# Attention and two expert layers on one core: one transposition for both heads' odd 64 keys, first keys by head, a planner that counts tiling changes and shared access, new ranks

## The chip, the cores and the metric

One core of a Trainium2 chip runs the whole program. The metric is the device time of one execution in microseconds (us). PE is the matrix engine, with PEld its weight loads; DVE, ACT and POOL are the vector, scalar and general engines, and SP issues most of the transfers. All engines work through their own instruction lists in order and wait for each other by semaphores.

## The reference

Attention over 2 batches of 8 heads, 576 positions, head size 64, in float32; its output goes through two expert layers.

```python
def _attn_ref(q, k, v):            # q, k, v: 2, 8, 576, 64
    ...
    q_rot, k_rot = (rotate(q), rotate(k))
    scores = (1.0 / np.sqrt(D)) * np.matmul(q_rot, k_rot.transpose(0, 1, 3, 2))
    attn = np.exp(scores - np.max(scores, axis=-1, keepdims=True))
    attn = attn / (np.sum(attn, axis=-1, keepdims=True) + 1e-09)
    return np.matmul(attn, v).astype(np.float32)

x = attn_out.transpose(0, 2, 1, 3).reshape(1152, 512)
h = x @ w_in;  x = (h * np.tanh(softplus(h))) @ w_out              # 512 -> 2048 -> 512
h = x @ w2_in; x = (P(h) / Q(h)) @ w2_out                          # the same sizes
```

## The kernel before

Attention goes pair by pair: eight pairs, each the two heads `2j` and `2j+1` of one batch. For a pair, `load` brings q, k and v, `turned` rotates q and k (`rope.1` to `rope.4`, on POOL for all pairs but the first, whose work is shared between DVE and POOL), and `columns` transposes them on PE and lets ACT and DVE split them into a high and a low part (`turn`, `turn.hi`, `turn.lo`). `score` multiplies queries by keys for a tile `t` of 128 query rows. For `t` 0 to 3 the two heads stand in the upper and lower 64 rows of PE and run side by side (12 matmuls of 288 columns); `t` = 4 holds the last 64 rows of both heads (6 matmuls over all 128 rows). DVE takes the row maxima (`score.max`), ACT the exponentials (`score.exp`). `turn_p` transposes the exponentials (`p.turn`), ACT and DVE take turns in copying the result out (`p.move`, `p.move2`), `weigh` multiplies it by the values, two heads in the two column halves of PE, and `shares` divides by the sums (`sum.turn`, `sum.spread`, `x.scale`, and `x.hi`, `x.lo` on POOL).

576 keys are four blocks of 128 and 64 odd ones. The four blocks of each head are transposed one by one; the odd 64 of the first head go to rows 0 to 63 of the transposed block `PTr`, those of the second head to rows 64 to 127, by two transpositions and two copies for each tile (L611, L612).

The expert layers follow (`up`, L807, and `down`, L891). Their weights come as 64-bit words, and `prepare` takes each half of a block apart: `w.size` (ACT), `w.bound`, `w.shift`, `w.low` (DVE), `w.hi` (ACT), `w.lo` (DVE). The first halves are prepared while attention still runs.

What sets the order is a planner, `Plan.emit`. Every operation has a cost in a table of formulas, and the planner plays the program through: of all operations that are ready it issues the one that can start first, after adding the operation's number in `YIELD`, and breaks ties by its place in the program plus its number in `EARLY_LATE`. It also hands out the eight PSUM banks (`Banks(1)`, `Banks(2)`). The order that comes out is fixed in the program.

Of the kernel before, what the change touches and what calls it, by code (L numbers as in the profile page):

```python
# [42 lines left out]
def pool(n, wide=False):  # L43
# [3 lines left out]

EARLY_LATE = {
    "down.add": 1136, "g.hi": -2317, "g.lo": 6461, "g.low": -15, "load": 762, "mish": 8083, "p.move": 2011,
    "p.turn": 31, "ratio.10": -108, "ratio.11": -2315, "ratio.2": -4968, "ratio.3": -593, "ratio.4": 423,  # L50
    "ratio.5": -1752, "ratio.6": 4202, "ratio.7": -3763, "ratio.8": 10584, "rope.1": -2749, "rope.2": 22,
    "rope.4": -2386, "score": -3812, "score.max": 3118, "start": -1592, "store": 1136, "sum.inv": 7595, "sum.lo":
    4253, "sum.row": 510, "sum.spread": -2329, "sum.turn": -7911, "turn": -370, "turn.lo": -3170, "up": -2124,
    "w.bound": -442, "w.hi": -117, "w.keep": -380, "w.lo": 426, "w.load": -689, "w.low": -124, "w.shift": -4497,
    "w.size": -2423, "weigh": 378, "x.hi": 924, "x.lo": 3178, "x.scale": 1155, "y.hi": 91, "y.lo": -3805}
# [4 lines left out]
    "down": 2368, "down.add": 703, "g.hi": 1295, "g.lo": 447, "g.low": 585, "mish": 850, "p.move": 218, "p.turn":  # L60
    481, "ratio.1": 120, "ratio.10": 228, "ratio.2": 48, "ratio.4": 2226, "ratio.5": 196, "ratio.6": 442,
    "ratio.7": 3284, "ratio.8": 485, "ratio.9": 549, "rope.1": 601, "rope.2": 1192, "rope.3": 501, "rope.4": 146,
    "score": 49, "score.max": 252, "sum.inv": 985, "sum.lo": 49, "sum.row": 196, "sum.spread": 430, "sum.turn":
    453, "turn.lo": 409, "up": 2286, "w.bound": 219, "w.hi": 859, "w.keep": 237, "w.lo": 1062, "w.load": 718,
    "w.low": 1007, "w.shift": 411, "w.size": 1921, "weigh": 1097, "x.scale": 105, "y.hi": 1745, "y.lo": 446}
# [16 lines left out]
class Plan:  # L82
# [3 lines left out]
    def __init__(self):  # L86
        self.ops = []
        self.write = {}
        self.reads = {}
        self.live = []  # L90
        self.turns = {}
        self.rank = []
        self.names = []

# [7 lines left out]
    def op(self, name, engine, cost, fn, r=(), w=(), late=0.0, after=()):  # L102
# [28 lines left out]
        self.names.append(name)  # L131
        self.ops.append((engine, cost, fn, deps, order - deps - {i}, late, banks))
        return i

    def emit(self, banks=8):
# [36 lines left out]
        users = {}  # L172

# [18 lines left out]
        while len(issued) < n:  # L192
            rooms = {}
            best = None
            for engine, group in ready.items():
                for i in group:
                    t = max(free[engine], at[i])
# [16 lines left out]
            issued.append(i)  # L214
            places = list(rooms[takes[i]][1]) if takes[i] else []
# [18 lines left out]
def block_kernel(ctx: ExitStack, tc: tile.TileContext, q, k, v, w1_in, w1_out, w2_in, w2_out,  # L234
# [211 lines left out]

    def load(p, n, queue=None):
# [6 lines left out]
        def main(h, e):  # L454
            i = src[b, 2 * j + h, 0:512, :]
            if n == "v":
                e.dma_start(out=vm[:, h].rearrange("p t d -> p (t d)"), in_=i.rearrange("(p t) d -> p (t d)", t=4))
            else:
                e.dma_start(out=t[:, 0:4, h, :], in_=i.rearrange("(p t) d -> p t d", t=4))  # L459

        def end(a, e):

            if n == "k":
                e.dma_start(out=last[0:64], in_=src[b, 2 * j:2 * j + 2, 512:S, :].rearrange("h p d -> p h d"))
            else:
# [9 lines left out]
        if p < 2:  # L475
            plan.op("start", "POOL", 300 if n == "k" else 600, zero, w=[(x, "z")])
        for h in range(2):
            dma([(x, h)], lambda e, h=h: main(h, e), 131e3, queue)
        for a in range(1 if n == "k" else 2):
            dma([(x, "e", a)], lambda e, a=a: end(a, e), 32e3 if n != "k" else 64e3, queue)  # L480
# [511 lines left out]
```

## Time and profile before

| | |
|---|---|
| time of three runs | median 576.4 us (576.3 to 576.94) |
| the profiled execution | 574.76 us, of which the span of the profile is 573.0 us |
| busy in the span | PE 547.1, PEld 495.2, DVE 459.1, ACT 373.4, POOL 102.5 us |
| busy in the chain that ended last | PE 89%, POOL 2%, DVE 2%, ACT 2% of the span |
| the expert layers' matmuls alone | L807 204.0 us and L891 201.9 us of PE |

The profiled execution is 1.76 us longer than its span, and 1.64 us shorter than the median of the runs. Until about 13 us the first keys and queries are loaded and turned, until about 175 us the eight pairs go through, and from there on the expert layers run.

### The profile page before, as it was taken

Reading aid. Unit: us, or ns where it says so; the run is one execution under the profiler, and the core shown is the slowest. Engines: PE = TensorE matmul, PEld = TensorE weight load, DVE = VectorE, ACT = ScalarE, POOL = GpSimd, SP = SyncE. Lnnn points to the kernel's source line nnn. Section 1 sums busy time; section 2 is a strip of 40 time slices with the busy share of each in tenths; the row PEclk is TensorE's granted clock in tenths of the full one; section 3 lists DMA queues with packets and bytes.
Section 4 is the critical chain, followed back from the end, with each engine's and each line's share of the span. In section 5 each row is a group of like instructions: output and inputs, shape, how many; then the busy total and the mean of one; then the engine's idle time right before and its main releaser. Section 6 shows DMA issues by size and latency. Waiting matters only on the chain.

```text
span 573.0 us, 8774 instructions
## 1 busy us (share of the span) xinstructions
PE 547.1 (95%) x3416; PEld 495.2 (86%) x3416; DVE 459.1 (80%) x629; ACT 373.4 (65%) x555; POOL 102.5 (18%) x100
## 2 busy tenths in 40 slices
PE   3998899799999999999999999999999999999997
PEld 2776676677689999999999999999998988999985
DVE  4778787877766866987876869789889989998993
ACT  2867584776766856686754788666765767655560
POOL 7979897302112000000000000000000000000000
PEclk9999899999999999999999999999999999999999
DMA  5434402201226192769292961503404300300004
GB/s 146 92 77 115 124 22 74 76 12 31 74 74 222 40 399 81 283 225 369 76 360 79 350 237 78 216 1 146 148 0 145 150 0 5 142 2 0 1 18 148
DMA packets 38681, 69.35 MB, mean 121 GB/s; under 512 B 22256, under 2 KB 24560, under 8 KB 37104
## 3 DMA queue, kind: packets, MB, share of 16 engines
q1 hardware_dynamic: 37296, 68.43, 34.2%
q8 instruction: 27, 0.44, 0.3%
q10 hardware_dynamic: 1344, 0.36, 0.3%
q14 instruction: 14, 0.11, 0.1%
HBM read 53.84 MB, written 14.94 MB: 120 GB/s over the span
## 4 chain that ended last, share of the span: by engine, by line
PE 89%; POOL 2%; DVE 2%; SPq 2%; ACT 2%; DMA 1%; issue 1%; POOLq 0%; DVEq 0%; ACTq 0%
PE banks L807 35%; PE banks L891 35%; PE banks L657 6%; PE banks L608 5%; PE banks L564 4%; ACT f L580 1%; DVE f L577 1%; PE banks L521 1%; PE banks L683 1%; POOL f L499 1%; SPq L466 1%; POOL f L500 1%; SPq L459 1%; PE banks L611 1%; PE banks L612 1%
## 5 line engine op out<-in xcount | busy, mean ns | idle before, releaser
L807 PE MATMUL banks<-r 128*128 128x384 f32 x1152 | 204.0, 334 | 0.0
L891 PE MATMUL banks<-r 128*128 128x384 f32 (+1 forms) x1008 | 201.9, 358 | 0.0
L807 PEld LDWEIGHTS banks<-r 128*128 128x128 f32 x1152 | 200.3, 188 | 0.8
L891 PEld LDWEIGHTS banks<-r 128*128 128x128 f32 x1008 | 181.0, 188 | 16.4
L580 ACT ACTIVATE f<-banks,f 128x576 f32<-128x576 f32 x72 | 52.9, 741 | 26.3 <-DVE f L577 25.6
L577 DVE TENSOR_REDUCE f<-banks 128x1 f32<-128x576 f32 x72 | 52.0, 751 | 17.7 <-PE banks L564 17.4
L564 PE MATMUL banks<-r 64*128 64x288 f32 (+1 forms) x432 | 45.8, 323 | 4.6 <-ACT f L580 3.7
L564 PEld LDWEIGHTS banks<-r 64*128 64x128 f32 (+1 forms) x432 | 36.9, 198 | 13.5 <-ACT f L580 6.0
L849 ACT ACTIVATE f<-banks 128x768 f32<-128x768 f32 x24 | 19.6, 815 | 44.1 <-PE banks L807 44.1
L897 DVE TENSOR_TENSOR x<-banks,x 128x384 f32<-128x384 f32 (+1 forms) x63 | 37.3, 610 | 10.3 <-PE banks L891 10.1
L657 PE MATMUL banks<-x,f 128*64 128x256 f32 (+1 forms) x320 | 42.4, 411 | 0.0
L833 DVE TENSOR_TENSOR r<-f,r 128x768 fp32r<-128x768 f32 x24 | 22.8, 957 | 22.1 <-ACT r L829 22.0
L630 DVE COPY x<-banks 128x512 f32<-128x512 f32 (+2 forms) x64 | 31.9, 504 | 10.6 <-PE banks L608 7.4
L608 PE MATMUL banks<-f 128*128 128x128 f32 x288 | 38.7, 277 | 1.5 <-ACT f L580 1.5
L854 DVE TENSOR_TENSOR f<-f 128x768 f32<-128x768 f32 x24 | 23.0, 959 | 17.5 <-ACT f L852 17.4
L332 ACT ACT_TABLE_LOAD x28 | 35.9, 1283 | 0.5
L608 PEld LDWEIGHTS banks<-f 128*128 128x128 f32 x288 | 31.6, 141 | 4.8 <-ACT f L580 2.0
L657 PEld LDWEIGHTS banks<-x,f 128*64 128x64 f32 x320 | 22.6, 136 | 14.2 <-issue 2.3
L626 ACT COPY x<-banks 128x512 f32<-128x512 f32 (+1 forms) x56 | 28.4, 525 | 9.3 <-PE banks L608 8.6
L829 ACT ACTIVATE f<-banks 128x768 f32<-128x768 f32 x24 | 19.4, 813 | 19.9 <-PE banks L807 19.8
L817 ACT CAST r<-f 128x768 fp32r<-128x768 f32 x24 | 19.5, 824 | 14.7 <-DVE f L865 14.7
L852 ACT ACTIVATE f<-f 128x768 f32<-128x768 f32 x24 | 24.7, 1030 | 2.3 <-DVE f L865 1.6
(78 smaller groups left out, 694.1 us busy)
## 6 DMA issues: line engine op xcount, KB each, us to landing
f<-in_moe_w_in SPq DMA_DIRECT2D x16, 1024.0 KB, 5.1
f<-in_moe_w_out SPq DMA_DIRECT2D x16, 1024.0 KB, 5.9
outside<-f SPq DMA_DIRECT2D x12, 1024.0 KB, 4.7
r<-outside SPq DMA_DIRECT2D x12, 1024.0 KB, 6.6
f<-in_v SPq DMA_DIRECT2D x16, 128.0 KB, 2.1
out<-x SPq DMA_DIRECT2D x8, 256.0 KB, 2.5
x<-in_k SPq DMA_DIRECT2D x14, 128.0 KB, 3.0
x<-in_q SPq DMA_DIRECT2D x8, 128.0 KB, 3.0
```

Source lines behind the costliest of these rows:

```text
L332: nc.scalar.preload_act_table_set(name)
L564: nc.tensor.matmul(bank(Ps[h])[:, hf, 0:HW], qT[r, x, t * 128:(t + 1) * 128], kT[r, y, hf * HW:(hf + 1) * HW], start=(n == 0), stop=(n == 2))
L577: nc.vector.tensor_reduce(nm, bank(P)[:, :, 0:HW], axis=AX.XY, op=ALU.max, negate=True)
L580: nc.scalar.activation(view(e.off, 2, HW), bank(P)[:, :, 0:HW], AF.Exp, bias=nm, accum_out=sm)
L608: nc.tensor.transpose(bank(P)[:, kb * 128:(kb + 1) * 128], x[:, kb * 128:(kb + 1) * 128], idf)
L626: nc.scalar.copy(o, i)
L630: nc.vector.tensor_copy(o, i)
L657: nc.tensor.matmul(bank(P)[64 * a:64 * a + 64, 0:n], l, r, start=(kb == 0), stop=(kb == 4), skip_group_check=True)
L807: nc.tensor.matmul(bank(P)[:, i, 0:BW], y[:, cb, f], x[:, cb, tok], start=(cb == 0 and n == 0), stop=(cb == CB - 1 and n == 2))
L852: plan.op("ratio.2", "ACT", act(N, False, 2), lambda: nc.scalar.activation(q_, a, AF.Identity, bias=prm[:, 4:5], scale=prm[:, 5:6]), r=[(b ...
L891: nc.tensor.matmul(bank(P)[:, 0:n], x, y, start=(f == 0 and j == 0), stop=(f == FT - 1 and j == 2))
L897: nc.vector.tensor_tensor(total(), bank(P)[:, 0:n], total(), ALU.add)
```

## The change

1. The exponentials of the two heads now lie side by side in one buffer of 1152 columns, so that the first head's last 64 keys and the second head's first 64 keys are neighbours. One transposition of these 128 columns and one copy fill `PTr` for both heads. The second head's blocks begin 64 keys later, and its values are loaded in the matching order, in four transfers where there was one and an end (`load`, `ENDS`).
2. The tile `t` = 4 is transposed in one group: ten transpositions of 64 rows, the two heads in the upper and lower rows of PE, into two banks (L664, L666, L667), where there were four of 128 and two odd ones.
3. The last 64 keys of a pair are transposed with all 128 rows instead of 64.
4. The first pair's keys are loaded head by head in one piece of 1 KB for each partition, one head by ACT's queue and one by SP's, and rotated head by head (`turned_first`); the first pair's other loads change queues, and the keys' end is transposed alone (`"f"`).
5. The planner adds 95 ns to an operation of PE whose tiling differs from the one before (`DIVIDE`, `form`), and lets no two operations of the list `SHARED` overlap. Some costs of PE's operations change with it.
6. `EARLY_LATE` and `YIELD` have other numbers throughout.

```diff
+DIVIDE = 95.0
+
+SHARED = {"rope.1", "rope.2", "rope.3", "rope.4", "x.hi", "x.lo", "w.bound", "w.shift", "w.low", "w.lo", "g.low", "g.lo", "ratio.3",
+          "ratio.9", "ratio.10", "ratio.11", "y.lo"}
...
-    "down.add": 1136, "g.hi": -2317, "g.lo": 6461, "g.low": -15, "load": 762, "mish": 8083, "p.move": 2011,
+    "down": 1720, "down.add": 895, "g.hi": -113, "g.lo": -913, "g.low": 4029, "load": 1697, "mish": 300, "p.move":
...
-                    t = max(free[engine], at[i])
+                    t = max(free[engine] + DIVIDE * (engine == "PE" and self.form[i] != divided), at[i])
+                    if names[i] in SHARED:
+                        t = max(t, shared)
...
-                e.dma_start(out=t[:, 0:4, h, :], in_=i.rearrange("(p t) d -> p t d", t=4))
+                e.dma_start(out=vm[:, h] if (n, p) == ("k", 0) else t[:, 0:4, h, :], in_=i.rearrange("(p t) d -> p t d", t=4))
...
+    def turned_first(x, b1, b2, engine):
...
+        for h in (1, 0):
+            for name, b, f in (("rope.1", b1, c), ("rope.2", b2, s)):
+                plan.op(name, engine, dve(256), lambda h=h, b=b, f=f: eng.tensor_tensor(
+                    view(b.off, 4, 4, 32)[:, :, 2 * h:2 * h + 2], view(x.off, 2, 4, 2, 32)[:, h], f, ALU.mult),
+                    r=[(x, h), ROPE_T], w=[(b, h)])
...
-        e = T["P", p, i] = plan.ring("P", PR, S, 6)
+        e = T["P", p, t] = plan.ring("P", PR, 2 * S, 3)
...
-            if a is not None:
-                x = view(es[a][0].off, S)
+            if t == 4:
+                x = view(es[0].off, 64 + S)
+                rs = slice(0, 64), slice(64, 128)
                 for kb in range(4):
-                    nc.tensor.transpose(bank(P)[:, kb * 128:(kb + 1) * 128], x[:, kb * 128:(kb + 1) * 128], idf)
+                    for h, r in enumerate(rs):
+                        nc.tensor.transpose(bank(P)[:, h, kb * 64:kb * 64 + 64],
+                                            x[r, 64 + 64 * h + kb * 128:64 + 64 * h + (kb + 1) * 128], idf[r, r])
+                nc.tensor.transpose(bank(P)[0:64, 0, 256:320], x[rs[0], S:S + 64], idf[rs[0], rs[0]])
+                nc.tensor.transpose(bank(P)[:, 1, 256:320], x[rs[1], 0:128], idf[rs[1], rs[1]])
                 return
-            for i in range(m):
-                nc.tensor.transpose(bank(P)[0:64, i * 128:(i + 1) * 128], view(es[0][i].off, S)[:, 512:S], idf)
-                nc.tensor.transpose(bank(P)[:, (m + i) * 128:(m + i + 1) * 128], view(es[1][i].off, S)[:, 448:S], idf)
+            for i, e in enumerate(es):
+                x = view(e.off, 2 * S)
+                k = [512] if a is None else [(S + 64) * a + kb * 128 for kb in range(4)]
+                for n, f in enumerate(k):
+                    nc.tensor.transpose(bank(P)[:, (i + n) * 128:(i + n + 1) * 128], x[:, f:f + 128], idf)
...
+        keys, last_keys = load(0, "k", nc.scalar)
+        queries, last_queries = load(0, "q", nc.scalar)
         dma([ROPE_T], lambda e: e.dma_start(out=tab, in_=rope), 164e3)
-        load(0, "k", nc.scalar)
-        load(0, "q")
-        dma([("idf",)], lambda e: e.dma_start(out=idf, in_=ident), 64e3, nc.scalar)
+        last_keys(0, nc.scalar)
+        keys(1, None)
+        keys(0, nc.scalar)
+        dma([("idf",)], lambda e: e.dma_start(out=idf, in_=ident), 64e3)
+        queries(0, nc.scalar)
+        queries(1, None)
```

How the rows move is read from the two programs' instruction lists. On PE, in the middle of attention of the program before: a run of 24 score matmuls, the spreading of the sums (L683, L685), transpositions of exponentials (L608, with L611 and L612 for the odd keys), and the next pair's keys and queries (L521).

```order
L564 MATMUL banks<-r 128x288 x24
L683 MATMUL banks<-r 128x128 x4
L685 MATMUL banks<-r 128x64 x2
L608 MATMUL banks<-f 128x128 x12
L611 MATMUL banks<-f 64x128
L612 MATMUL banks<-f 128x128
L611 MATMUL banks<-f 64x128
L612 MATMUL banks<-f 128x128
L564 MATMUL banks<-r 128x288 x12
L521 MATMUL banks<-f,x 128x128 x9
L521 MATMUL banks<-f,x 128x64
```

A pair's round in the changed program, a little earlier in attention (L618 are the score matmuls, L673 all transpositions of whole tiles, L664 to L667 those of `t` = 4, L571 those of keys and queries, L719 the product with the values):

```order
L618 MATMUL banks<-r 128x288 x24
L673 MATMUL banks<-f 128x128 x14
L618 MATMUL banks<-r 128x288 x18
L673 MATMUL banks<-f 128x128 x8
L664 MATMUL banks<-f 128x64 x8
L666 MATMUL banks<-f 64x64
L667 MATMUL banks<-f 128x64
L673 MATMUL banks<-f 128x128 x4
L571 MATMUL banks<-f,x 128x128 x10
L719 MATMUL banks<-x,f 64x256 x10
```

The pairs of L611 and L612 are gone, the group of ten for `t` = 4 stands behind a run of 18, and all ten transpositions of the next pair's keys and queries have 128 rows.

On ACT, at the start of the program before (loads of the first keys, of the identity, the table of functions, and the first split):

```order
L459 DMA x<-in_k 128x4x64 x2
L464 DMA x<-in_k 64x2x64
L712 DMA f<-c_ident 128x128
L713 ACT_TABLE_LOAD
L530 ACTIVATE r<-banks 128x512
```

In the changed program:

```order
L782 ACT_TABLE_LOAD
L481 DMA x<-in_k 128x256
L481 DMA x<-in_q 128x4x64
L486 DMA x<-in_k 64x2x64
L583 ACTIVATE r<-banks 128x64
```

The table of functions is now loaded ahead of the three transfers, the keys' end is third, and the first split is that of the keys' end; the second head of the keys stands second in SP's list.

On DVE, where the second half of the first expert weights is taken apart during attention (L394 `w.bound`, L397 `w.shift`, L400 `w.low`), the program before has:

```order
L630 COPY x<-banks 64x64 x2
L394 TENSOR_SCALAR f<-f 128x1024
L577 TENSOR_REDUCE f<-banks 128x1
L397 TENSOR_SCALAR f<-f 128x1024
L400 SCALAR_TENSOR_TENSOR f<-f 128x1024
L577 TENSOR_REDUCE f<-banks 128x1 x4
```

The same three steps in the changed program (L410, L413, L416; L632 are the maxima, L752 is `x.scale`, L759 `sum.lo`):

```order
L632 TENSOR_REDUCE f<-banks 128x1 x2
L759 TENSOR_TENSOR r<-banks,r 9x128
L410 TENSOR_SCALAR f<-f 128x1024
L413 TENSOR_SCALAR f<-f 128x1024
L416 SCALAR_TENSOR_TENSOR f<-f 128x1024
L632 TENSOR_REDUCE f<-banks 128x1
L752 TENSOR_TENSOR f<-f,banks 128x576
```

They have moved from the fifth pair's maxima to those of the seventh pair, and stand in one piece.

## Rows read from the trace of the kernel before

**Rows 1.** Busy time by stretch: each engine's busy us and instructions, PE's granted clock, DMA.

```profile
12.98:171.00 158.02, 146.09 (x1242) 114.35 (x1242) 121.68 (x210) 107.75 (x261) 89.94 (x71) 0.99 0.25 68
50.00:64.00 14.00, 9.71 (x75) 7.80 (x75) 12.11 (x18) 8.02 (x19) 13.61 (x11) 0.88 0.34 100
175.00:390.00 215.00, 215.00 (x1238) 214.45 (x1238) 169.26 (x215) 150.82 (x161) 3.48 (x2) 1.00 0.55 204
```

**Rows 2.** Timeline of PE, 33.5 to 39 us: start us, duration us, instruction, idle before.

```profile
34.08 1.85 PE L564 MATMUL banks<-r 64*128 64x288 f32 x24
36.95 0.94 PE L521 MATMUL banks<-f,x 128*128 128x128 f32 x6 [1.02 <-POOL f L503]
```

**Rows 3.** Costliest groups: count, busy us, mean ns of one, idle before them.

```profile
L580 ACT ACTIVATE f<-banks,f 128x576 f32<-128x576 f32 x72 | 52.9, 741 | 26.3 <-DVE f L577 25.6
```

**Rows 4.** Timeline of DVE and PE around 100 us, then DVE at 137 us.

```profile
97.81 1.25 DVE L397 TENSOR_SCALAR f<-f 128x1024 int32<-128x1024 int32 x1
...
99.09 2.46 DVE L400 SCALAR_TENSOR_TENSOR f<-f 128x1024 int32<-128x1024 int32 x1
...
103.14 0.66 PE L683 MATMUL banks<-r 128*128 128x128 f32 x4 [2.96 <-ACT f L580]
...
137.37 0.68 DVE L397 TENSOR_SCALAR f<-f 128x1024 int32<-128x1024 int32 x1
```

**Rows 5.** Timeline of PE at 60 us.

```profile
60.46 3.40 PE L564 MATMUL banks<-r 128*128 128x288 f32 x18 [2.17 <-ACT f L580]
```

**Rows 6.** Timeline of PE, 25 to 30 us.

```profile
25.08 0.27 PE L521 MATMUL banks<-f 128*128 128x128 f32 x1
25.29 0.27 PE L521 MATMUL banks<-f,x 64*128 64x64 f32 x1
...
28.25 1.04 PE L608 MATMUL banks<-f 128*128 128x128 f32 x8
29.12 0.27 PE L611 MATMUL banks<-f 128*64 128x128 f32 x1
...
29.65 1.07 PE L564 MATMUL banks<-r 64*128 64x288 f32 x12
```

**Rows 7.** Timeline of the first 13 us, all engines and queues.

```profile
0.75 1.32 ACTq L459 DMA_DIRECT2D x<-in_k  x2
...
2.10 0.65 ACTq L464 DMA_DIRECT2D x<-in_k  x1
...
3.44 1.28 ACT L713 ACT_TABLE_LOAD   x1 [3.44 <-issue]
...
5.29 0.69 DVE L499 TENSOR_TENSOR f<-x,f 128x512 f32<-128x512 f32 x1 [4.32 <-DMA x<-in_k]
...
7.57 0.50 POOL L501 TENSOR_TENSOR x<-f 128x64 f32<-128x64 f32 x1
...
7.92 0.43 DVE L499 TENSOR_TENSOR f<-x,f 128x256 f32<-128x256 f32 x1
...
7.95 1.12 PE L521 MATMUL banks<-f,x 128*128 128x128 f32 x4 [7.95 <-DMA f<-in_q]
...
10.06 0.68 DVE L536 TENSOR_TENSOR r<-banks,r 128x512 fp32r<-128x512 f32 x1
...
12.98 3.25 PE L564 MATMUL banks<-r 64*128 64x288 f32 x24
```

**Rows 8.** Issues of transfers: count, size of each, median us from issue to landing.

```profile
f<-in_moe_w_out SPq DMA_DIRECT2D x16, 1024.0 KB, 5.9
...
f<-in_v SPq DMA_DIRECT2D x16, 128.0 KB, 2.1
...
x<-in_k ACTq DMA_DIRECT2D x2, 128.0 KB, 3.2
```

**Rows 9.** Timeline of PE at the end of attention.

```profile
167.38 4.44 PE L807 MATMUL banks<-r 128*128 128x384 f32 x24
171.75 2.38 PE L657 MATMUL banks<-x,f 128*64 128x256 f32 x20
```

More of the change, by code (lines that the diff above doesn't have):

```diff
@@ L52 @@
[L52 to L55, printed above, removed]
-YIELD = {
[L60 to L65, printed above, removed]
+    "down": 1720, "down.add": 895, "g.hi": -113, "g.lo": -913, "g.low": 4029, "load": 1697, "mish": 300, "p.move":
@@ new lines @@
+    458, "p.turn": 3152, "ratio.1": -256, "ratio.10": 1560, "ratio.11": 519, "ratio.2": -70, "ratio.3": 3622,
+    "ratio.4": -1438, "ratio.5": 1161, "ratio.6": -1346, "ratio.7": 5516, "ratio.8": -122, "ratio.9": -499,
+    "rope.1": 622, "rope.2": 4908, "rope.4": 6139, "score": 1181, "score.exp": 806, "score.max": -3148, "sum.inv":
+    -547, "sum.lo": -606, "sum.row": 49, "sum.spread": -1239, "sum.turn": 1357, "turn": 4458, "turn.hi": -3984,
+    "turn.lo": 458, "w.keep": 163, "w.lo": 80, "w.load": 1068, "w.low": -283, "w.shift": 440, "w.size": -230,
@@ new lines @@
+    "weigh": -1239, "weigh.move": 1181, "x.hi": 1214, "x.lo": -7147, "y.hi": 1383, "y.lo": 1882}
+YIELD = {
+    "down": 8354, "down.add": 127, "g.hi": 389, "g.low": 896, "load": 3676, "p.move2": 507, "p.turn": 456,
+    "ratio.2": 430, "ratio.4": 619, "ratio.7": 1445, "ratio.8": 370, "ratio.9": 26, "rope.1": 510, "rope.2": 523,
+    "rope.3": 540, "rope.4": 609, "score.max": 246, "start": 568, "sum.inv": 87, "sum.lo": 803, "sum.spread": 337,
+    "sum.turn": 242, "turn": 730, "turn.lo": 5, "up": 7594, "w.bound": 322, "w.hi": 1182, "w.lo": 1177, "w.load":
+    901, "w.low": 792, "w.shift": 15, "w.size": 1278, "weigh": 920, "weigh.move": 191, "x.hi": 285, "x.lo": 635,
+    "x.scale": 79, "y.hi": 186, "y.lo": 863}
@@ L100, in ring, with op @@
         return Buf(off + n * (i % size), n)
-    def op(self, name, engine, cost, fn, r=(), w=(), late=0.0, after=()):
+    def op(self, name, engine, cost, fn, r=(), w=(), late=0.0, after=(), form=""):
         i = len(self.ops)
@@ L172, in emit @@
         users = {}
+        divided, shared = "", 0.0
         def room(ws):
@@ L214, in emit @@
             issued.append(i)
+            if names[i] in SHARED:
+                shared = end
+            if engine == "PE":
+                divided = self.form[i]
             places = list(rooms[takes[i]][1]) if takes[i] else []
@@ L464, in end @@
                 e.dma_start(out=last[0:64], in_=src[b, 2 * j:2 * j + 2, 512:S, :].rearrange("h p d -> p h d"))
+            elif n == "v" and a:
+                i = src[b, 2 * j + 1, 0:256, :].rearrange("(p t) d -> p t d", t=4)
+                x = (vm[64:128, 1, 0:3, :], vm[64:128, 1, 3, :], last[64:128, 1, :])[a - 1]
+                e.dma_start(out=x, in_=(i[:, 1:4, :], src[b, 2 * j + 1, 512:S, :], i[:, 0, :])[a - 1])
             else:
@@ L593, in turn_p @@
     def turn_p(p, a, t):
[L597 removed]
+        P = Banks(2 if t == 4 else 1)
         main, rest = places(p)
         c = slice(main.start + t * 128, main.start + (t + 1 + (a is None)) * 128) if t < 4 else rest
[L600 to L602 removed]
+        es = [T["P", p, i] for i in ((t, t + 1) if a is None and t < 4 else (t,))]
```

114 lines of the change are left out of this document (68 added, 46 removed).

## The prediction

> **What bounds the kernel now.** I read the busy time by stretch first. From 175 to 390 us PE is busy without a gap [rows 1], and the rest of the expert layers is the same chain of matmuls. The change takes no matmul out of them, so I look for the gain ahead of 175 us. From the first score at 12.98 us to 171 us PE is busy for 146.09 of 158.02 us, idle for 11.9 [rows 1]: attention is bound by PE too, but with holes. DVE is busy for 121.68 us there and ACT for 107.75, so neither is full on the average.
>
> Next I read the timeline for what ends the holes; there are three kinds. First, 24 score matmuls in one run fill all eight banks of PSUM (four tiles of two). After such a run PE has to wait until an exponential has emptied a bank: the run that starts at 34.08 us is over at 35.93, and PE goes on at 36.95 after 1.02 us of idling [rows 2]. The row names POOL; that operation only ended close by, and what frees a bank is an exponential on ACT, 0.74 us each [rows 3]. Second, preparing the experts' weights on DVE holds up the maxima. The shift alone takes 0.68 us, but 1.25 us while POOL rotates, and the step behind it 2.46; PE then waits 2.96 us for an exponential [rows 4]. Third, after such a hole of 2.17 us 18 matmuls took 3.40 us [rows 5]; the clock granted from 50 to 64 us is 0.88 of the full 2.4 GHz [rows 1], which is what about 3.4 of the 14 us at the lower level, 1.2 GHz, would give. That costs half of 3.4, 1.7 us. Holes and low clock together are 11.9 + 1.7 = 13.6 us.
>
> **The change, part 1: PE's instructions.** A transposition costs 0.109 us of PE: eight of them from 28.25 to 29.12 us [rows 6]. The odd keys of a pair took eight such for the tiles 0 to 3 and now take four: 4 x 0.109 x 8 pairs = -3.5 us. The copies halve as well; ACT and DVE have room, so I count them at nothing on the average. If DVE were full they would be worth a little more.
>
> The tile `t` = 4 took six transpositions, 0.65 us, and takes ten of 64 rows now. No row shows a transposition of 64 rows by 128. The nearest are the score matmuls in half rows: 12 take 1.07 us [rows 6] and 24 take 1.85 [rows 2], so one adds 0.065. Eight at 0.065 and the two uneven ones at 0.109 make 0.74, or +0.09 a pair, +0.7 in all. If both heads ran side by side perfectly, ten would cost five halves of 0.109 and a little, 0.33 (-2.6 in all); if nothing overlapped, 1.09 (+3.5).
>
> A change of tiling costs about 0.1 us: the transposition of 64 rows at 25.29 us stands 0.21 behind its forerunner, where neighbours of one tiling stand 0.11 apart [rows 6]. Counting scores in half rows, weighing in half columns and transpositions of 64 rows as tilings of their own, I find 85 changes in PE's old order and 81 in the new one: the keys' ends lose 16, the groups of ten bring 8 and the new ranks 4. That is -0.4 us. The Trainium skill (TensorEngine Tiling (Array Packing), Key Properties) says that changing the tiling mode drains PE, and that switching only between tiles does not. It speaks against the ten small transpositions, which put a mode of their own between whole ones; the trace agrees, with 0.1 us for each change, so by the rule too these groups cost 0.8 us of what they are for.
>
> Part 1: -3.5 + 0.7 - 0.4 = -3.2 us, between -6.5 and 0.
>
> **Part 2: the start.** Two loads of the keys, issued by ACT from 0.75 to 2.07 us, end DVE's first wait at 5.29 [rows 7]. A load of that size in 256-byte pieces lands 3.2 us after its issue, and the values, which have the layout that the keys get now, 2.1 [rows 8]. With the two heads in the first slots of two queues both are there at about 1.4 + 2.1 = 3.5 us, and DVE, which needed from 5.29 to 7.92 for the rotation, ends at about 6.3 (four products in the place of two cost two more starts). The keys' first transposition hardly gains, though. PE's order now begins with the keys' end, which POOL rotates; its load is third in ACT's list as before (2.10 us), and POOL was through at 8.07 [rows 7]. The whole keys follow at about 8.1, against 7.95. What gains is the queries: DVE rotates them right behind the keys, for 2.1 us (7.92 to 10.06 [rows 7]), and is through at 8.4 instead of 10.06. So keys and queries are transposed and split in one go, and the other tiles' transpositions are behind the first scores, not ahead of them. I put four rows of split behind one another (0.25 + 0.6 on ACT, 0.68 + 0.42 on DVE, by the 0.68 of the whole keys [rows 7] and shares of it) and come to 11.1 us for the first score: -1.9 us. At best POOL, with DVE no longer beside it, ends 0.7 us sooner: -2.6.
>
> The lower bound is the table of functions. It takes 1.28 us on ACT [rows 7] and now stands ahead of ACT's three loads; before, it stood behind them, so no row shows whether a load waits for it. If it does, the first head and the keys' end come 1.3 us later and the start is worth 0.6. I take the case that it doesn't. The Trainium skill (Perfetto Trace Analysis, DVE / Act Engine Instruction) has the sequencer ready for the next instruction as soon as one is pushed to the engine's wait queue, so by it the loads go out at once and the start is worth 1.9; no run here shows it yet.
>
> **Part 3: the holes.** Here the order decides. In the new order of PE I count seven runs of 24 and seven of 18 score matmuls. At the old price of 1.02 us [rows 2] the former cost 7.1 us. Behind the latter each group of four transpositions, 0.44 us, follows an exponential of 0.74; most of that is covered by what lies between, and I take 0.3 us a run, 2.1. The second half of the weights is now taken apart at the seventh pair, when POOL's rotations have ended; but the first half's `w.low` stands at the fifth pair, where POOL still rotates, and delays two maxima: 1.0 us, which is 2.46 [rows 4] less about twice the 0.68 that a step takes alone. At the end of attention the 24 expert matmuls of 167.38 us filled the wait for the last exponentials' copies [rows 9]; in the new order no expert matmul stands ahead of the last product with the values, and the third half's two passes on DVE (0.7 each) stand ahead of the last copies: 1.5 us. Sum 7.1 + 2.1 + 1.0 + 1.5 = 11.7, and I expect no low clock. Against 13.6 that is -1.9 us. Bounds: the holes fall to 7 (-6.6), or every run of either kind waits 0.4 longer than I think (+3.7).
>
> The values' loads become six for a pair instead of four; SP's list issues them a pair ahead, and a landing takes 2.1 us [rows 8] while a pair takes some 20. If the cover went, the first product with the values would wait about 2 us. The expert layers: the fourth half of the weights is loaded only after the third is taken apart, at the end of attention. Its chain (a landing of 5.9 us [rows 8], then six passes of ACT and DVE, 7.5 us at the 1.25 of the slow shift [rows 4]) must end before the first `down`, which is four runs of 24 expert matmuls later, 4 x 4.37 = 17.5 us by the two starts of [rows 9]; 4 us to spare, so nothing. If that cover went, `down` would wait for the rest of the 13.4 us.
>
> **Sum.** -3.2 - 1.9 - 1.9 = -7.0 us. The span goes from 573.0 to 566.0, the profiled execution (1.76 longer) to 567.8, and the median of runs, which lay 1.64 above the profiled execution, to about **569.4 us**.
>
> **Rivals.** *The loads wait for the table.* For it: one list, in order. Against it: nothing measured. The start is worth 0.6 instead of 1.9: 570.7 us.
>
> *The shared access was the larger loss.* If keeping DVE's weight steps off POOL's rotations also shortens the copies and rotations all along, the holes fall to 7: 569.4 - 4.7 = 564.7 us. For it: 1.25 against 0.68 us for one operation, and both large holes lie behind such steps [rows 4, 5]. Against it: the first half's three steps stay beside POOL's rotations in the new order, and the third half's stand in the last stretch, where the copies that end attention wait.
>
> *Given back.* PE's saved time becomes waiting, since ACT and DVE have to do nearly the same work in less time. With DVE busy for 121.68 of then about 151 us, 81%, the maxima come later behind each run; if the 5.1 us of parts 1 and 3 go that way, only the start is left of the gain, and with a lost 0.6 us of it 575.1 us or a little more: no measurable change.
>
> *Slower: the banks.* In PE's new order five of the seven runs of 24 are followed by something that needs two neighbouring banks (the spreading of the sums, or the group of ten), and the DVE work of the pair before comes due there. If each waits like the spreading at 103.14 us, 2.96 instead of 1.02 [rows 4, 2], that is 7 x 1.94 = 13.6 us more: 583.0. It turns the result from 1.0 us more for each run (7.0 / 7). Against it: most runs of 24 had holes of about 1 us, and 2.96 had `w.low` ahead of the maxima.
>
> *The count of tiling changes does nothing*: it falls by 4 of 85; the forecast has this already.
>
> **How the numbers follow.** The measurement can tell about 0.2%, 1.15 us, from no change. Chances: the forecast 0.50 (its own range 566 to 573), loads wait 0.12, shared access 0.15, given back 0.13, slower 0.10. Faster by over 0.2% (below 575.2): 0.50 + 0.12 + 0.15 and half of given back, 0.83. Within 0.2%: 0.07. Slower: 0.10. The range from 564.0 to 575.5 leaves out the slower case, a little of given back above and under half of the shared-access case below, about 0.2.
>
> **What would show it.** Part 1: the group of whole transpositions loses 32 of odd keys, and a group of ten lasts about 0.75 us. Part 2: DVE's first product starts near 3.5 us, ACT's first load is issued near 0.8 (not 2.1), the first score starts near 11.1. Part 3: PE's idle time from the first score to the last product with the values is near 11.7 us, its holes about 1 us each behind runs of 24, the granted clock 1.00 throughout. The prediction is wrong if holes of 2 to 3 us stand behind the runs of 24, if the first `down` waits for its weights, or if a group of ten takes over 1.1 us.

## The result, and the profile after

The changed kernel takes 562.2 us (median of four runs, 561.87 to 562.56) against 576.67 us for the kernel before in the same session: a ratio of 0.9746, with a 95% interval of 0.9729 to 0.9763. That is 14.5 us, twice the 7.0 that were forecast, and below the range. The span went from 573.0 to 560.0 us, 13.0 us less; the rest of the 14.5 is that the profiled execution of the kernel before (574.76) lay 1.9 us below this median, and that of the changed kernel (561.87) 0.3 below its own. Readers can follow where the 13.0 us of the span come from in three stretches: the start, attention, and the expert layers.

The start, in the timeline of all engines (columns as in [rows 7]):

```profile
0.74 1.28 ACT L782 ACT_TABLE_LOAD   x1 [0.74 <-PEq L1048]
...
0.78 0.39 ACTq L481 DMA_DIRECT2D x<-in_k  x1
...
1.87 0.64 ACTq L486 DMA_DIRECT2D x<-in_k  x1
...
4.30 1.43 DVE L523 TENSOR_TENSOR f<-x,f 128x256 f32<-128x256 f32 x4 [3.34 <-DMA x<-in_k]
...
7.11 0.49 POOL L553 TENSOR_TENSOR x<-f 128x64 f32<-128x64 f32 x1
...
7.66 1.76 PE L571 MATMUL banks<-f,x 128*128 128x128 f32 x7 [7.66 <-POOL x L553]
...
8.27 0.28 DVE L553 TENSOR_TENSOR x<-f 128x128 f32<-128x128 f32 x1
...
9.02 0.87 ACT L583 ACTIVATE r<-banks 128x512 fp32r<-128x512 f32 x2 [0.63 <-PE banks L571]
9.65 0.69 DVE L589 TENSOR_TENSOR r<-banks,r 128x512 fp32r<-128x512 f32 x1 [0.97 <-ACT r L583]
9.95 3.55 PE L618 MATMUL banks<-r 64*128 64x288 f32 x24 [0.53 <-ACT r L583]
```

The first score starts at 9.95 us in place of 12.98 [rows 7]. ACT issued its first load at 0.78 while the table was being loaded from 0.74 to 2.02, so the loads did not wait for it. The rule of the Trainium skill that the prediction cited (Perfetto Trace Analysis, DVE / Act Engine Instruction) agrees with that.

Attention, from the first score to the first expert matmul: busy time of PE by stretch (us, PE busy with its instructions, granted clock, DMA share, GB/s). The first row is of the kernel before and holds 24 expert matmuls of 4.37 us that stand inside attention there [rows 9]; the second is of the changed kernel.

```profile
12.98:174.75 161.77, 149.84 (x1272) 0.99 0.25 69
```

```profile
9.95:157.66 147.71, 138.07 (x1249) 1.00 0.26 71
```

Without those 4.37 us attention went from 157.40 to 147.71 us: 9.7 us less. Idle time fell from 11.93 to 9.64, the clock no longer drops, and the rest, 7.4 us, is busy time. Adding up in the timeline of PE, for each matmul, the distance from its start to the start of the next, less the idle time between them, shows which: the transpositions of the exponentials went from 43.82 to 39.23 us (-4.6), and the score matmuls, the same 432, from 44.40 to 41.28 (-3.1). Of these 3.1 the low clock of [rows 5] explains 1.3 (3.40 us there, 2.02 to 2.10 for such a run in the changed kernel); the other 1.8 are runs that took longer without an idle time on record, such as the two of 18 in 2.5 us that start at 20.82 and 121.52 in the kernel before, at a granted clock of 1.00. What held them up the trace doesn't say. Products with the values and the transpositions of keys and queries took 0.3 us more together. The expert layers took 0.3 us less.

The score matmuls in the two pages, before and after:

```profile
L564 PE MATMUL banks<-r 64*128 64x288 f32 (+1 forms) x432 | 45.8, 323 | 4.6 <-ACT f L580 3.7
L618 PE MATMUL banks<-r 64*128 64x288 f32 (+1 forms) x432 | 42.6, 315 | 1.3 <-ACT f L635 0.7
```

The timeline of PE in the changed kernel, a run of 24 and a group of ten, and the end of attention:

```profile
31.05 1.87 PE L618 MATMUL banks<-r 64*128 64x288 f32 x24
33.90 0.66 PE L745 MATMUL banks<-r 128*128 128x128 f32 x4 [0.98 <-ACT f L635]
...
36.56 2.02 PE L618 MATMUL banks<-r 128*128 128x288 f32 x18
38.52 1.09 PE L673 MATMUL banks<-f 128*128 128x128 f32 x8
39.54 0.46 PE L664 MATMUL banks<-f 64*128 64x64 f32 x8
39.84 0.22 PE L666 MATMUL banks<-f 64*64 64x64 f32 x1
39.84 0.22 PE L667 MATMUL banks<-f 64*128 64x64 f32 x1
40.00 0.66 PE L571 MATMUL banks<-f,x 128*128 128x128 f32 x4
...
43.35 0.28 PE L755 MATMUL banks<-f 128*9 128x128 f32 x1 [1.06 <-DMA x<-in_q]
...
157.47 0.36 PE L747 MATMUL banks<-r 128*128 128x64 f32 x2
157.66 16.90 PE L877 MATMUL banks<-r 128*128 128x384 f32 x96
174.40 1.89 PE L961 MATMUL banks<-r 128*128 128x384 f32 x10
```

A run of 24 is followed by a hole of 0.98 us, as before; a run of 18 by none. The group of ten takes 0.46 us from its start to the next operation. The hole of 1.06 us at 43.35 is a new one: the transposition of a pair's sums (L755) comes right behind DVE's reciprocals, which end at 43.30; the load that the row names only landed close by. After the last product there is no hole, and the first `down` (L961) does not wait.

### The profile page after: what moved, and what is told of

Read it like the earlier page. It is cut to its first block, busy times and chain, and to the rows that moved or that the text cites. A ratio compares the mean times of both kernels' runs of the same rounds, so it can differ in the third digit from the quotient of the medians.

```text
span 560.0 us, 8769 instructions
## 1 busy us (share of the span) xinstructions
PE 538.2 (96%) x3416; PEld 488.2 (87%) x3416; DVE 452.4 (81%) x618; ACT 366.8 (65%) x548; POOL 96.2 (17%) x100
## 4 chain that ended last, share of the span: by engine, by line
PE 90%; DVE 4%; ACT 3%; DMA 2%; issue 1%; POOL 0%; DVEq 0%; ACTq 0%; POOLq 0%; SPq 0%
PE banks L877 36%; PE banks L961 35%; PE banks L719 7%; PE banks L618 5%; PE banks L673 4%; DVE f L632 2%; ACT f L635 2%; PE banks L571 1%; DVE x L690 1%; PE banks L745 1%; DMA x<-in_q 1%; DMA f<-in_q 1%; DMA f<-c_rope 1%; DVE f L413 0%; DVE f L752 0%
## 5 line engine op out<-in xcount | busy, mean ns | idle before, releaser
L961 PE MATMUL banks<-r 128*128 128x384 f32 (+1 forms) x1008 | 201.6, 358 | 0.0
L961 PEld LDWEIGHTS banks<-r 128*128 128x128 f32 x1008 | 180.9, 188 | 16.4
L632 DVE TENSOR_REDUCE f<-banks 128x1 f32<-128x576 f32 x72 | 51.1, 752 | 19.9 <-PE banks L618 19.2
L967 DVE TENSOR_TENSOR x<-banks,x 128x384 f32<-128x384 f32 (+1 forms) x63 | 38.2, 610 | 13.6 <-PE banks L961 13.5
L618 PE MATMUL banks<-r 64*128 64x288 f32 (+1 forms) x432 | 42.6, 315 | 1.3 <-ACT f L635 0.7
L719 PE MATMUL banks<-x,f 128*64 128x256 f32 (+1 forms) x320 | 42.6, 411 | 0.3 <-DMA f<-in_q 0.2
L618 PEld LDWEIGHTS banks<-r 64*128 64x128 f32 (+1 forms) x432 | 34.8, 192 | 8.5 <-issue 3.0
L673 PE MATMUL banks<-f 128*128 128x128 f32 x288 | 39.6, 278 | 2.6 <-ACT f L635 2.1
L673 PEld LDWEIGHTS banks<-f 128*128 128x128 f32 x288 | 31.2, 140 | 8.7 <-ACT f L635 4.9
L719 PEld LDWEIGHTS banks<-x,f 128*64 128x64 f32 x320 | 23.5, 136 | 13.9 <-issue 1.7
L690 DVE COPY x<-banks 128x512 f32<-128x512 f32 (+2 forms) x52 | 28.7, 571 | 5.4 <-PE banks L673 5.0
L686 ACT COPY x<-banks 128x512 f32<-128x512 f32 (+2 forms) x52 | 24.6, 500 | 9.2 <-PE banks L673 6.2
L929 ACT ACTIVATE f<-f 128x768 f32<-128x768 f32 x24 | 22.4, 935 | 6.4 <-DVE f L924 5.2
```

The source lines that it names most:

```text
L618: nc.tensor.matmul(bank(Ps[h])[:, hf, 0:HW], qT[r, x, t * 128:(t + 1) * 128], kT[r, y, hf * HW:(hf + 1) * HW], start=(n == 0), stop=(n == 2))
L632: nc.vector.tensor_reduce(nm, bank(P)[:, :, 0:HW], axis=AX.XY, op=ALU.max, negate=True)
L673: nc.tensor.transpose(bank(P)[:, (i + n) * 128:(i + n + 1) * 128], x[:, f:f + 128], idf)
L686: nc.scalar.copy(o, i)
L690: nc.vector.tensor_copy(o, i)
L719: nc.tensor.matmul(bank(P)[64 * a:64 * a + 64, 0:n], l, r, start=(kb == 0), stop=(kb == 4), skip_group_check=True)
```

## The experiments

Each ran in four rounds beside the kernel before, whose median lay between 576.9 and 578.2 us in these sessions; medians are given, against the changed kernel's 562.2, which was not measured again in them. A difference of under 1 us or so is therefore read from attention in the profile, and with caution. Below, "attention" is the time from the first score to the first of the long expert runs in the profile, 147.71 us in the changed kernel. The first score itself falls between 9.8 and 10.5 us in the kernels that keep the changed start, by when the load of the keys' end lands (5.3 to 5.9 us), so I compare attention and not ends.

### Code and order exchanged

The first run is the changed kernel with the old planner and its old tables; the second is the kernel before with the new ones.

```diff
-DIVIDE = 95.0
-SHARED = {"rope.1", "rope.2", ...}
+DIVIDE = 0.0
+SHARED = set()
...
-        plan.op("weigh", "PE", 10 * 0.82 * n + 15, pe, r=src, w=[(P,)], form="columns")
+        plan.op("weigh", "PE", 10 * 0.82 * n + 200, pe, r=src, w=[(P,)], form="columns")
```

with `EARLY_LATE` and `YIELD` as they were.

> The changed kernel with the planner as it was: the old two tables of numbers, the old costs of score, weigh and sum.spread, no cost for a change of tiling, nothing kept apart on shared access. Theory A (the order removed the holes, the low clock and the stalls inside the runs of scores; the edits of the instructions did the rest): the 2.3 us of idle time and 3.0 us of longer score runs come back, about 567.5 us, idle time in attention near 12 us, the start unchanged near 9.95. Theory B (fewer copies and transpositions emptied the holes whatever the order): within 1 us of 562.2. Theory C (the new instructions need the new order): 570 or more, above what the sum of the parts gives.

> The kernel before with the new planner and its two new tables, everything else as before. Theory A: it loses the same 5.3 us, to about 571.4 us. Theory B: the order alone is worth under 1 us, so 575.5 to 577. Theory C: slower than 576.7, since the numbers were made for other operations.

Measured: 589.4 and 576.6 us. In the first run the old tables lose 27.2 us with the new code, as theory C has it, and 17.0 of them lie in the expert layers, where PE stands idle for 10.8 us. The second is no different from the kernel before (576.88 in its session, the ratio between 0.9977 and 1.0008): that is theory B. In its profile the first score starts only at 15.35 us, 2.4 later than before, and attention takes 157.34 us, where the kernel before takes 157.40 without its 24 expert matmuls. Neither number is the price of a part. In the first run `down` (L958 there) sits idle for weights, as the groups of PE show:

```profile
L958 PE MATMUL banks<-r 128*128 128x384 f32 x576 | 105.2, 341 | 6.9 <-ACT r L423 4.2 <-DVE r L427 2.7
```

To take the parts apart, the next runs fix the order: the planner takes, of the operations that are ready, the one that stands first in a list taken from the other kernel.

```diff
-                    if best is None or (t, rank[i], i) < best:
-                        best = t, rank[i], i
+                    if best is None or ORDER[i] < best[1]:
+                        best = t, ORDER[i], i
```

### The changed code in the old order

> The changed kernel's instructions and start, all else issued in the order of the kernel before (the planner takes, of what is ready, the operation that stood first there). Theory A (the order removed holes, low clock and stalls by itself): 2.3 us of idle time and 3.0 us of longer score runs come back, 567 to 568 us. Theory B (with fewer transpositions and copies any order has fewer holes): under 563.5. Theory C (each order fits only the operations it was made for, as the 589.4 and 576.6 us of the two exchanged tables suggest): 570 or more.

Measured: 577.1 us, theory C again. The holes of before are back (2.40 us ahead of the score run at 59 us, 2.33 at 101), and the fewer copies did not close them.

Laid side by side, the new planner and tables with the old instructions (576.6 us) and the new instructions in the old order (577.1) both stand where the kernel before stands, and only the two together give 562.2. So the gain is no sum of one part for the instructions and one for the order.

### The start alone

The loads, queues, rotation and first transpositions of before, the rest in the new order:

```diff
-        keys, last_keys = load(0, "k", nc.scalar)
-        queries, last_queries = load(0, "q", nc.scalar)
+        load(0, "k", nc.scalar)
+        load(0, "q")
...
-        if (n, p, ts.start) == ("k", 0, 0):
-            return turned_first(x, b1, b2, engine)
```

> The changed kernel with the start as before (loads, queues, rotation and first transpositions of the first pair), the rest in the changed order. Theory A (the start's gain goes through to the end): first score near 13.0, plus 3.0 us, 565.2. Theory B (the first holes take it up): plus 1 us or less.

Measured: 564.65 us, 2.45 more, with the first score at 12.99 and attention at 147.53. Most of the start's gain goes through to the end (theory A): 2.45 of the 3.04 us between 9.95 and 12.99, where other kernels with the changed start begin as late as 10.5.

The start has one wait left: PE's first transposition follows POOL, whose keys' end is third in ACT's list. One run exchanges the second and the third load in the list of the order.

> The changed kernel, same order, but ACT issues the load of the keys' end ahead of that of the first head's queries. Theory A (the first transposition waits for POOL, which waits for this load): it lands 0.6 us sooner, the first score starts at 9.4 to 9.7, minus 0.3 to 0.6 us, 561.7. Theory B (then the rotation of the other keys on DVE ends last): no change.

Measured: 562.18 us. The first score moved to 9.56, as theory A has it, but attention took 148.44, so nothing is left of it at the end.

### The weights' steps put back

PE's order stays word for word; only the loads and the steps of ACT and DVE that take the expert weights apart return, in the list of the order, to where they stood among the maxima.

> The changed kernel with the steps that take the first experts' weights apart (ACT, DVE and their loads) moved back to where they stood before among the maxima, PE's order unchanged. Theory A (beside POOL's rotations these steps take up to 2.5 us in the place of 0.7 to 1.2, hold up the maxima and made the two large holes and the low clock behind one): holes of 2 to 3 us at two places, plus 3 to 6 us, 565 to 568. Theory B (the order of the runs on PE decides, the place of these steps does not): plus 1 us or less.

Measured: 570.7 us, 8.5 more; attention 157.01. This is theory A, and more than it gave. DVE and POOL in its timeline (L488 is `w.bound`, L491 `w.shift`, L494 `w.low`; L627 to L629 are POOL's rotations, L843 its `x.lo`):

```profile
54.00 1.54 POOL L627 TENSOR_TENSOR f<-x,f 128x640 f32<-128x640 f32 x1
54.05 2.04 DVE L488 TENSOR_SCALAR f<-f 128x1024 f32<-128x1024 f32 x1
...
55.49 1.98 POOL L628 TENSOR_TENSOR f<-x,f 128x640 f32<-128x640 f32 x1
...
56.68 1.35 DVE L491 TENSOR_SCALAR f<-f 128x1024 int32<-128x1024 int32 x1
...
57.44 1.85 POOL L843 TENSOR_TENSOR r<-f,r 128x576 fp32r<-128x576 f32 x1
...
58.06 2.31 DVE L494 SCALAR_TENSOR_TENSOR f<-f 128x1024 int32<-128x1024 int32 x1
59.25 1.83 POOL L629 TENSOR_TENSOR x<-f 128x320 f32<-128x320 f32 x1
...
61.96 2.34 PE L696 MATMUL banks<-r 128*128 128x288 f32 x8 [2.68 <-ACT f L713]
```

The two engines take turns by whole instructions, as far as these rows show. The shift starts at 56.68 and ends at 58.03, 0.6 us after POOL's rotation ended at 57.47; `w.low` starts at 58.06 and ends at 60.37, 1.1 us after POOL's ended at 59.29. The maxima behind them come late, PE is idle for 2.68 us, and its clock falls (us, PE busy, granted clock, DMA share, GB/s):

```profile
56.00:60.00 4.00, 1.75 (x8) 0.69 0.00 0
60.00:64.00 4.00, 2.04 (x8) 0.50 0.62 180
```

To part the two engines from the place, the next run keeps that place, but POOL waits for `w.low` by copying one column of its result.

```diff
+                if plan.hold:
+                    plan.op("w.hold", "POOL", 100, lambda n=n: nc.gpsimd.tensor_copy(tiny[:, 8:9], view(CUT[n], 1024)[:, 0:1]), r=[val], w=[("hold",)])
```

> As the run with the weights' steps back at their old place, and POOL now copies one column of their result before it goes on rotating, so it stands still while DVE takes the first two halves apart. Theory A (what cost 8.5 us there was DVE and POOL standing in each other's way): the steps take 0.7, 0.7 and 1.2 us, the hole of 2.7 us and the low clock are gone, 563.5 to 566. Theory B (the place among the maxima is what costs): 569 or more, with the steps short and the holes there.

Measured: 567.05 us, attention 152.68. In its timeline (L489, L492 and L495 are the three steps, L713 the maxima):

```profile
54.68 0.68 DVE L489 TENSOR_SCALAR f<-f 128x1024 f32<-128x1024 f32 x1
...
55.95 0.69 DVE L492 TENSOR_SCALAR f<-f 128x1024 int32<-128x1024 int32 x1
...
56.67 1.23 DVE L495 SCALAR_TENSOR_TENSOR f<-f 128x1024 int32<-128x1024 int32 x1
...
57.96 0.18 POOL L517 COPY f<-f 128x1 f32<-128x1 f32 x1 [3.26 <-DVE f L495]
...
59.48 3.13 PE L699 MATMUL banks<-r 128*128 128x288 f32 x18 [1.59 <-ACT f L716]
```

The steps have their short times, and 3.6 of the 8.5 us are gone. So keeping the two engines apart gave 3.6 us back, and 4.9 us stay with the place among the maxima: a hole of 1.59 us where the changed kernel has 0.23, and still a run of 18 mostly at half clock (3.13 us in place of 2.02 to 2.10; granted 0.57 from 60 to 64 us). In the 4.9 is also what it costs that POOL stands idle for 3.26 us and rotates later, which no run takes apart. Both theories hold in part.

### The transpositions put back

Before's transpositions of the exponentials and its loads of the values, in the new order:

```diff
-        e = T["P", p, t] = plan.ring("P", PR, 2 * S, 3)
+        e = T["P", p, i] = plan.ring("P", PR, S, 6)
...
-                if t == 1 or t == 3:
-                    add(at + 1.1, turn_p, p, None, t - 1)
+                if t != 0 and t != 2:
+                    add(at + 1.1 * (t < 4), turn_p, p, None, t - (t < 4))
```

> The changed kernel with the transpositions of the exponentials as before (odd keys by head, the tile 4 in two groups, the values loaded as before), in the changed kernel's order; start and keys' end as changed. Theory A (the saved instructions are worth their time on PE): 4.6 us of transpositions come back, 566.8. Theory B (as in the run with the odd keys twice, some 60% of PE's added time shows): plus 2.8, 565.0. Theory C (the copies, 8 more for a pair, hold up the maxima on DVE and the holes grow): 568 or more.

> As the run with the transpositions of before in the changed order (573.5), but each copy goes to the engine that has it in the changed kernel; the extra group of the tile 4 uses the engine of its neighbour. Theory A (11.3 us there were mostly instructions on PE and the 8 added copies a pair): 571 or more. Theory B (part of it was that the copies sat on other engines than the order was made for): 569 or less.

Measured: 573.5 and 569.8 us; attention 158.82 and 155.31. The second run differs in one line, which decides whose turn it is to copy:

```diff
-        T["moves"] = T.get("moves", 0) + 1
+        T["moves"] = T.get("moves", 0) + ((a, t) != (None, 4))
```

So 3.7 of the 11.3 us came from copies on engines that the order was not made for. The other 7.6 us are what the edit is worth in this order. The copies added are two for a pair (120 in place of 104), and not the eight of these expectations. By the sums over PE's timeline (143.3 us busy in attention against 138.1, 12.0 idle against 9.6) about two thirds of the 7.6 are PE's time and one third are holes. Three runs, all in exactly the changed order, look at its pieces. The odd keys twice on PE:

```diff
-                for n, f in enumerate(k):
+                for n, f in list(enumerate(k)) * (2 if a is None else 1):
```

> The changed kernel with each transposition of the odd keys of the tiles 0 to 3 issued twice (the second overwrites the first with the same numbers): 4 more for a pair, 32 in all, at 0.109 us. Theory A (PE's instructions set the time of attention one for one): plus 3.5 us, 565.7. Theory B (they fall into holes, as the saved ones of before would have): plus 1 us or less. This measures what taking 32 of them away was worth.

Two copies of 64 rows in the place of one of 128:

```diff
-                return [(PTr[:, c], x[:, 0:m * 128])]
+                return [(PTr[64 * h:64 * h + 64, c], x[64 * h:64 * h + 64, 0:m * 128]) for h in range(2)]
```

> The changed kernel, same order and the same instructions on PE, but the odd keys' transposed block is copied out in two copies of 64 rows in the place of one of 128: 16 copies more over ACT and DVE, some 0.4 us each. Theory A (the copies that the change saved were worth time: what waits behind one are maxima and exponentials, which free PSUM's banks for PE): plus 2 to 4 us, 564 to 566. Theory B (ACT and DVE have room for them, as the prediction counted): plus 0.5 us or less.

The heads of the tile 4 one after the other:

```diff
-                for kb in range(4):
-                    for h, r in enumerate(rs):
+                for h, r in enumerate(rs):
+                    for kb in range(4):
```

> The changed kernel with the eight small transpositions of the tile 4 written head after head instead of in turns; the order of all else is the same. Theory A (in turns, the two heads run side by side in the upper and lower rows of PE, which is why eight take 0.30 us): a group of eight takes 0.5 to 0.9 us and the time grows by 1.8 to 4.6 us, to 564.0 to 566.8. Theory B (they are short because they have 64 rows and columns): no change, 562.2. In between, if some of it hides in holes.

Measured: 564.26 us with the odd keys twice (attention +2.5), 563.82 with two copies (+1.6), 562.63 with the heads apart (+0.4). Of 3.5 us of PE some 60 to 70% show at the end, the rest falls into holes (between A and B). The copies are not free: 1.6 us, between A and B too. Writing the heads in turns does nothing: eight small transpositions take 0.30 us either way, the time of B. But the reason of A is not refuted, for the halves ran side by side in both. In the changed kernel the ten start in pairs, under 0.02 us apart, and a pair comes every 0.06 us (a whole one every 0.109); written head after head they start in the same pairs. One group of that run shows that the halves don't wait for each other. Its program issues eight L664, then L666 in the upper rows, then L667 in the lower, and L666 started ahead of the last L664:

```profile
86.20 0.40 PE L664 MATMUL banks<-f 64*128 64x64 f32 x7
86.44 0.22 PE L666 MATMUL banks<-f 64*64 64x64 f32 x1
86.44 0.22 PE L664 MATMUL banks<-f 64*128 64x64 f32 x1
86.50 0.22 PE L667 MATMUL banks<-f 64*128 64x64 f32 x1
```

### The planner's two rules

The list of shared access emptied:

```diff
-SHARED = {"rope.1", "rope.2", ...}
+SHARED = set()
```

> The changed kernel, planned without keeping the listed operations of DVE and POOL apart (the list is empty), so with another order from the middle of attention on. Theory A (this rule is what keeps the weights' steps short): some of these steps take over 1.3 us again and the time is 3 us or more above 562.2. Theory B (the numbers of the tables alone hold them apart): within 1 us.

No price for a change of tiling; two more runs have the same line with 96.0 and with 90.0:

```diff
-DIVIDE = 95.0
+DIVIDE = 0.0
```

> The changed kernel, planned without the 95 ns for a change of tiling, so with 8 more rows in PE's order. Theory A (a change of tiling costs PE 0.1 us and no more hangs on it): plus 1 us or less. Theory B (the tables' numbers fit only the order they were found with): plus 2 us or more, in holes that have nothing to do with tiling. Theory C (the rule does nothing): no change.

> The changed kernel, planned with 96 ns in the place of 95 for a change of tiling, a difference that stands for nothing on the chip but moves 17 rows of PE's order and more on DVE and ACT. Theory A (the tables' numbers fit one order, and any other that the planner falls into is worse): plus 4 us or more, so that the runs without the two planner rules say little about these rules. Theory B (orders near this one are as good): within 1.5 us, and the 7 to 8 us of those runs belong to the rules.

> The same with 90 ns, which moves other rows, 9 or 10 on each of PE, ACT and DVE. Theory A: plus 2 us or more. Theory B: within 1.5 us.

Measured: 569.3, 570.7, 572.7 and 563.6 us. The third run decides how the first two are to be read: one nanosecond more in a cost moves 17 rows of PE's order and costs 10.5 us. There, attention is 2.9 us longer, and then the first `down` waits for weights that were taken apart too late, and goes on at a low clock (granted 0.66 from 180 to 190 us):

```profile
182.94 1.01 PE L961 MATMUL banks<-r 128*128 128x384 f32 x2 [4.27 <-ACT r L426]
```

With 90 ns it costs 1.4 us. So orders near this one may be as good or much worse, and the 7.1 and 8.5 us of the first two runs can't be booked as the worth of the rules. What the run without the list does show is slow steps again: `w.lo` took 1.66 us on the average, 1.22 in the changed kernel. Slow steps need not cost that much: with 90 ns `w.shift` took 1.27 us on the average, 0.97 in the changed kernel, and the time is only 1.4 us longer.

## Why the prediction was wrong

The direction and the places were right; the sum missed half. Of the 7.2 us between 569.4 and 562.2, part 3 missed 3.5, part 1 1.4 and part 2 1.1; the last 1.2 are the step from the span to the median, put at the old 3.4 us (1.76 and 1.64), where 2.2 were measured. By its own steps:

**Part 1, PE's instructions: forecast -3.2, measured -4.6 us.** The odd keys came as forecast (-3.5; 32 issued twice added 3.6 to PE's whole transpositions). The term that was mis-sized is the group of ten: it was put at 0.74 us and takes 0.48 on the average, 0.46 in the rows above, where the six of before took 0.65 at 0.109 each. That is -1.4 instead of +0.7. The bound named (ten at 0.33, both heads side by side) was nearer, and its reason agrees with the trace: five pairs at 0.06 make 0.30, and 0.1 to 0.2 more goes at the change back to whole ones. The price of 0.065 for one was that of a score matmul, and about half of it would have been right. A change of tiling costs what was forecast (the last whole transposition ahead of a group of ten takes 0.20 us and not 0.11), but no run prices the 0.4 us for having fewer of them.

**"The copies halve as well; ACT and DVE have room, so I count them at nothing on the average."** This step failed. In the changed order 16 copies put back cost 1.6 us, and about a third of the 7.6 us of the whole edit is idle time of PE. An average over attention (121.68 us of DVE in 158, [rows 1]) says nothing of the moments at which PE waits for an exponential and that for a maximum behind a copy.

**Part 2, the start: forecast -1.9, measured -3.0 us**, and 2.45 by the run that puts it back. The keys were there at 4.30, not 3.5 (their two loads took 3.0 and 3.1 us to land, not 2.1), but POOL ended at 7.60, not 8.07, and DVE at 8.55, near the 8.4 expected. The splitting was over-priced: the first scores need only the high parts of both, so PE starts at 9.95 while DVE still makes the low ones; the run then takes 3.55 us and not 3.25 [rows 7].

**Part 3, the holes: forecast 13.6 to 11.7, measured 13.2 to 9.6 (the low clock cost 1.3, not 1.7), and 1.8 us inside the score runs gone as well, for which the prediction had no term.** This step failed by the most. Runs of 24 cost a little less than forecast (six of seven have 0.82 to 0.98 us, the first 0.27, 6.0 in all; 7.1 were put down). Of the three other terms, 4.6 us together, those for `w.low` and for the end of attention (1.0 and 1.5) were not there at all, and behind runs of 18 there are a few holes of 0.2 us in place of 2.1 us. What makes up the 9.6 are holes that the prediction didn't name: 1.06 us ahead of the sums' transposition at 43.35, 0.45 and 0.27 ahead of score runs, and many short ones. For `w.low` the prediction looked at where the step stood in DVE's list and took it that POOL goes on rotating beside it. It overlooked that POOL can stand still there. It did, for 10.60 us, until DVE's `x.scale` released it:

```profile
84.20 1.22 DVE L416 SCALAR_TENSOR_TENSOR f<-f 128x1024 int32<-128x1024 int32 x1
...
93.33 1.15 POOL L763 TENSOR_TENSOR r<-f 128x576 fp32r<-128x576 f32 x1 [10.60 <-DVE f L752]
```

In the changed kernel `w.low` took 1.22 us on the average in attention:

```profile
L416 DVE SCALAR_TENSOR_TENSOR f<-f 128x1024 int32<-128x1024 int32 x3 | 3.7, 1219 | 0.0
```

Before it took 2.46 beside POOL [rows 4]. The rival "the shared access was the larger loss" had this, at 564.7 us and a chance of 0.15, though the holes did not fall to its 7 us. The runs that put it back cost 8.5 us with the place among the maxima, the most of any, and 3.6 of them went when the two engines were kept apart. Its "against" was the same mistake. The list does not keep the engines apart everywhere: at 151.84 us of the changed kernel `w.shift` still took 1.79 us beside POOL's `x.lo`, 1.83.

**The range** reached to about one bound at a time, and all three parts came out on the same side. The other rivals fell: the loads did not wait for the table, little was given back, and no run of 24 cost 2.96 us. The "4 us to spare" ahead of the first `down` were there in this order, but not in every other: in the runs with 96 ns and with the old tables that wait is there.

Put back one by one, start, weights' steps and transpositions cost 2.45 + 8.5 + 7.6 = 18.6 us, more than the whole gain of 14.5. The prices do not add. That each order was fitted to its own operations would explain this and the two times near 577 us, but no run shows it by itself, and what the order is worth alone stays open.

## What to carry to other kernels

Where an order was found by search, exchange parts with the order held fixed, and first change a cost by a nanosecond to see how much a mere other order is worth; here it was 10.5 us. An engine with room on the average is not free: look at what stands behind its operations at the moments when the engine that sets the time waits. Before an operation on DVE is priced, look at what POOL does beside it, in the new order and not in the old.

## What the runs showed of the hardware

In these traces DVE's passes over SBUF of 1024 columns and POOL's rotations exclude each other by whole instructions: 0.68, 0.69 and 1.23 us with POOL held off, 2.04, 1.35 and 2.31 beside it, and POOL's own rotations grew too, from 1.55 to 1.98 and from 0.86 to 1.83. The Trainium skill (SBUF — State Buffer, SBUF: two separate sides) calls the pair of ports that they share an exclusive lock, held by one instruction to its end. The rows above agree.

Transpositions of 64 rows in the two halves of PE's rows started in pairs, one pair every 0.06 us, where whole ones come every 0.109, and they did so in either order of writing. What a series in one half alone would take, no run shows.
